# Ranks two steps behind the rows, logits' parts taken out of the bank by ScalarE, eight groups of row blocks, up to two row scatters a step, and the leading expert's weights asked for behind all of v

## The chip, the cores and the metric

The kernel runs on one core of a Trainium2 chip. The time is the device time of one execution in microseconds (us), the median of several runs. A profile is one further execution under the hardware profiler; its span, 430.7 us, goes from the first to the last instruction.

Names in the profile: PE is TensorE's matmuls, PEld its weight loads, DVE is VectorE, ACT is ScalarE, POOL is GpSimd, SP is SyncE, which here issues the loads. A "bank" is one of the eight banks of PSUM, the memory that TensorE writes.

## The reference

Gated linear attention first, one recurrence per batch and head, over 768 tokens with head dimension 48, for 4 batches and 8 heads:

```
state = alpha[t][:, None] * state + outer(k[t], v[t])
y[t]  = q[t] @ state
```

The results are laid out as 3072 rows of 384 numbers, `x`. Then comes a router with eight experts, of which each row takes one:

```
logits = normalised(x) @ normalised(expert_emb).T / tau
expert = argmax(logits);  gate = softmax(logits)[expert]
out[row] = gate * (relu(x[row] @ w1[expert]) @ w2[expert])
```

`w1` is 384 x 1024 and `w2` 1024 x 384 for each expert; everything is fp32.

## The kernel before

**Two stages.** The attention stage works in 24 chunks of 128 tokens (`NS` = 24, six to a batch). A pipelined loop of 27 steps `s` runs over them: step `s` starts chunk `s`, does the scores of chunk `s - 1`, and finishes chunk `s - 2`. The expert stage then goes through the experts in turn. The leading one is chosen at run time from those that have at least 256 rows after 16 chunks, so that its first 256 rows can be worked on early (`fetch_early`, `turn_early`, `first_layer_early`, in steps 24 to 26).

**A step.** `decays` transposes alpha, k and q on TensorE into banks (`pa`, `pk`, `pq`). VectorE scans alpha backwards (`r`, L480), multiplies k by it (`kr`, L487), and in `decay_queries` scans alpha forwards (`a`, L504). GpSimd multiplies q by that (`qs`, L508). `keys_back` turns `kr` of the chunk before back (`pkb`, then `kb` by ScalarE, L525). `scores` multiplies keys by queries and masks (VectorE one half; ScalarE copies the other, L573, and GpSimd masks it, L574). `decay_state` (`dec`, L533, GpSimd) and `update` (`pd`; `state`, L558, VectorE) carry the state on. The first chunk of each batch has no carried state, so two steps later TensorE has fewer products. `mix_states` and `mix_chunk` form the outputs by columns (`pyx`, then `ycols` by ScalarE, L613), and `rows` (L615) turns them into rows.

**Rows and logits.** In `rows` the matrix `sel` holds unit columns and the scaled expert embeddings, so the product `px` gives in one bank both the rows (2 x 48 columns in each of four parts) and the logits' parts (8 columns in each). VectorE adds the four parts up (L633), and ScalarE copies the rows (L637). Both write into `x`, a tile for a whole group of chunks; its columns from `LG` on are the logits, and column `TK` is the token's number.

**Banks.** `pa`, `pk`, `pq`, `pkb` and `px` share three banks (`ps_tr`). A product can start when a bank is free, which is when all who read the tile that was in it are done. `pd` and the ranks' product `rk` share one (`ps_mm`).

**Routing.** Chunks are gathered into groups (`GROUPS`). One step after the last rows of a group are due, so at the end of step `last + 2`, `choose` (L325) finds the expert of each row on VectorE: five operations over the group, then the running count `before`, one addition per chunk on GpSimd (L342), on VectorE for chunks 15 and 23. A step later, at `last + 3`, `place` (L344) gets the rank of each row among the rows of its expert: two products with a triangle and a matrix of ones into `rk`, a multiplication (L364), a sum (L366) and a conversion to whole numbers (L367), which gives `dest`. `to_rows` (L312) then scatters one chunk's rows to DRAM at `dest` by an indirect DMA that GpSimd issues (L313); `send` is the list of chunks that wait for it, and inside the loop one chunk a step is sent. After chunk 15, `place` also gives the counts to `first_expert` (L375), a chain of small VectorE operations that ends in `turn_i` and `row0`.

**Order.** TensorE's order is written out: `in_turn()` puts each product behind the last. `behind(s)` puts work behind the forward scan on VectorE and behind `qs` on GpSimd. The rest of each engine's order is fixed when the kernel is built, by a planner that goes by program order and its own estimates of when inputs are ready.

**Loads.** `load(s)` (L447) asks SyncE's queue for alpha, k and q of chunk `s` and v of chunk `s - 1`; it is called two steps ahead, and four buffers (five for v) limit how far transfers run ahead. `weights(i)` (L135) asks for the two matrices of the expert that is `i`-th in turn; it reads the number from `turn_i` first. `weights(0)` is asked for right after `fetch_early()`, behind the scatter of chunk 15, and `weights(1)` at step 23.

Of the kernel before, what the change touches and what calls it, by code (L numbers as in the profile page):

```python
# [9 lines left out]
FP32 = mybir.dt.float32  # L10
I32 = mybir.dt.int32
AF = mybir.ActivationFunctionType
ALU = mybir.AluOpType
AX = mybir.AxisListType
# [13 lines left out]
def kernel(  # L28
# [12 lines left out]
    nc = tc.nc  # L41
    B, H, S, D = q.shape
# [16 lines left out]
    LG, TK, ROW = DM, DM + E, DM + E + 1  # L59

    GROUPS = (
        (0, 3), (3, 6), (6, 9), (9, 12), (12, 14), (14, 16), (16, 19), (19, 21), (21, 23), (23, 24)
    )
    GMAX = max(b - a for a, b in GROUPS)

# [130 lines left out]
    def in_turn():  # L196
        return tc.issue_after(last["pe"].ins) if last else ExitStack()


    with ExitStack() as c1:  # L200
# [143 lines left out]
        def place(g, total=False):  # L344

            s0, s1 = GROUPS[g]
            n = s1 - s0
            ch = chosen[:, s0:s1]
            bank = ps_mm.tile([P, GMAX + 1, E], FP32, tag="mm", name="rk")
            rk = bank[:, 0:n]  # L350
            rkf = rk.rearrange("p s e -> p (s e)")
            mm(
                rkf, lhsT=ones, rhs=before[:, s0:s1].rearrange("p s e -> p (s e)"),
                start=True, stop=False,
            )
            mm(
                rkf, lhsT=earlier, rhs=ch.rearrange("p s e -> p (s e)"),
                start=False, stop=True,
            )
            if total:  # L360

                mm(bank[:, GMAX], lhsT=ones, rhs=before[:, s1], start=True, stop=True)
            at = work.tile([P, GMAX, E], FP32, name="at_row")[:, 0:n]
            nc.vector.tensor_tensor(at, rk, ch, ALU.mult)  # L364
            row = work.tile([P, GMAX], FP32, name="row")[:, 0:n]
            nc.vector.tensor_reduce(row.unsqueeze(2), at, axis=AX.X, op=ALU.add)  # L366
            nc.vector.tensor_copy(dest[:, s0:s1], row)  # L367
            send.extend(range(s0, s1))
            if not total:
                return None  # L370
            m = work.tile([P, E], FP32, name="n")
            nc.vector.tensor_tensor(m, bank[:, GMAX], ebase, ALU.subtract)
            return m
# [73 lines left out]
        def load(s):  # L447

            if s < NS:
                b, c = divmod(s, NCH)  # L450
                i = s % NBUF
                for p0, p1 in ((1, AROW), (AROW, P)):
                    nc.sync.dma_start(out=at_s[i][p0:p1, :, 0:D], in_=a_r[b, c, p0:p1])
                nc.sync.dma_start(out=kt_s[i][:, :, 0:D], in_=k_r[b, c])
                nc.sync.dma_start(out=qt_s[i][:, :, 0:D], in_=q_r[b, c])
            if s > 0:
                b, c = divmod(s - 1, NCH)
                nc.sync.dma_start(out=vt_s[(s - 1) % NBV][:, :, 0:D], in_=v_r[b, c])

        def behind(s):  # L460

            queue = ExitStack()
            for call in st[s]["last"]:
                queue.enter_context(tc.issue_after(call.ins))
            return queue
# [149 lines left out]
        def rows(s):  # L615

            yT = st[s]["yT"]
            px = ps_tr.tile([P, 2, NQ, 2 * D + E], FP32, tag="tr", name="px")
            for hh in range(2):
                for q in range(NQ):  # L620

                    for i in range(2):
                        sl = slice(i * HALF, (i + 1) * HALF)
                        mm(
                            px[sl, hh, q], lhsT=yT[hh][:, q, sl], rhs=sel[:, hh, q],
                            start=True, stop=True, skip_group_check=True,
                        )
            g = group_of[s]
            s0, s1 = GROUPS[g]
            if s == s0:  # L630
                x_g[g] = work.tile([P, GMAX, ROW], FP32, name="x", bufs=4)[:, 0 : s1 - s0]
            x = x_g[g][:, s - s0]
            nc.vector.tensor_reduce(  # L633
                x[:, LG : LG + E].unsqueeze(2), px[:, :, :, 2 * D :].rearrange("t a q e -> t e a q"),
                axis=AX.XY, op=ALU.add,
            )
            nc.scalar.copy(  # L637
                x[:, 0:DM].rearrange("t (q j a d) -> t a q j d", q=NQ, j=2, a=2),
                px[:, :, :, 0 : 2 * D].rearrange("t a q (j d) -> t a q j d", j=2),
            )  # L640


# [21 lines left out]
        def warm(n):  # L664

            pw = ps_mm.tile([P, P], FP32, tag="mm", name="pw")
            for _ in range(n):
                mm(pw, lhsT=ident, rhs=ident, start=True, stop=True)

        send = []  # L670
        warm(7)
        fixed_parts()
        load(0)
# [2 lines left out]
        load(1)  # L676
        for s in range(NS + 3):
            if s + 2 <= NS:
                load(s + 2)
            if 0 <= s - 1 < NS:  # L680
                with in_turn():
                    keys_back(s - 1)
            if s < NS:
                decays(s)
            if s == NS:
                with in_turn():
                    turn_early()
            if s < NS:
                decay_queries(s)
            if 0 <= s - 1 < NS:  # L690
                decay_state(s - 1)

                with in_turn(), tc.issue_after(st[s]["a_scan"].ins) if s < NS else ExitStack():
                    scores(s - 1)
            if s == 0:
                with behind(s), in_turn():
                    prepare_first(a0)
                with behind(s):
                    prepare_logits()
            if NS <= s < NS + 2:  # L700
                with in_turn():
                    first_layer_early(2 * (s - NS), 2 * (s - NS) + 1)
            if 0 <= s - 2 < NS:
                with in_turn():
                    mix_states(s - 2)
                with in_turn():
                    mix_chunk(s - 2)
            if 0 <= s - 1 < NS:

                with in_turn(), tc.issue_after(st[s]["a_scan"].ins) if s < NS else ExitStack():  # L710
                    update(s - 1)
            if 0 < s < NS and s % NCH == 0:

                with in_turn():
                    keys_back(s, ps_mm, "mm")
            if NS <= s < NS + 2:
                with in_turn():
                    first_layer_early(2 * (s - NS) + 1, 2 * (s - NS) + 2)
            if 0 <= s - 2 < NS:
                with in_turn():  # L720
                    rows(s - 2)
            if s == 1:
                with in_turn():
                    turn_logits()
            if s == 2:
                with behind(s):
                    routing_constants()
            if s == 3:
                with behind(s):
                    convert_constants()  # L730
            if 4 <= s < 4 + NXG * (NC + 1):
                i, t = divmod(s - 4, NC + 1)
                with behind(s):
                    nc.gpsimd.memset(xg_s[i][:, t], 0.0)
            if s == 3:
                with behind(s):
                    nc.gpsimd.memset(blank, 0.0)

            r = s - 3
            if r >= 0:  # L740
                g = group_of[r]
                if r == GROUPS[g][1] - 1:
                    with in_turn():
                        n = place(g, r in (S0 - 1, NS - 1))
                    if r == S0 - 1:
                        with behind(s):
                            first_expert(n)
            with behind(s) if s < NS else ExitStack():
                for c in send[:] if s >= NS else send[:1]:
                    to_rows(dest[:, c : c + 1], x_g[group_of[c]][:, c - GROUPS[group_of[c]][0]])  # L750
                    send.remove(c)
                    if c == S0 - 1:
                        fetch_early()
                        weights(0)
            if s == NS - 1:
                weights(1)
            r = s - 2
            if 0 <= r < NS:
                g = group_of[r]
                if r == GROUPS[g][1] - 1:  # L760
                    choose(g)
                    with behind(s) if s < NS else ExitStack():
                        nc.gpsimd.tensor_copy(x_g[g][:, :, TK], toks[:, slice(*GROUPS[g])])
            if s > NS:
                with in_turn():
                    first_layer_early(2 * (s - NS) + 2, 2 * (s - NS) + 4)
# [483 lines left out]
```

## Time and profile before

Three runs: 432.58, 432.67 and 433.79 us.

| what | value |
|---|---|
| median time | 432.67 us |
| span of the profile | 430.7 us |
| busy: PE, PEld | 412.2, 361.2 us |
| busy: DVE, ACT, POOL | 280.9, 174.6, 192.4 us |
| attention loop, first alpha transpose of chunks 0 to 23 | 4.7 to about 141.5 us |
| first early product of the leading expert | 149.25 us |
| TensorE's granted clock, mean | 0.996 |

Busy time is the sum of an engine's instructions, so TensorE's 412.2 of 430.7 us says that it has nearly always something in hand. Its matmuls are pipelined, and the ends shown are modelled; the weight loads, one before each product, are therefore the better clock of what it does. In the timeline, a line gives start and length in us, the engine, the line of the kernel, the operation, what it writes and reads, and how many instructions of the kind it merges; in brackets stands the idle time of the engine ahead of it, and what ended that. In the list of waits, a line gives the waiting engine with its operation, the one it waited for, the total in us, how often, and the longest.

### The profile page before, as it was taken

Reading aid. Unit: us, or ns where it says so; the run is one execution under the profiler, and the core shown is the slowest. Engines: PE = TensorE matmul, PEld = TensorE weight load, DVE = VectorE, ACT = ScalarE, POOL = GpSimd, SP = SyncE. Lnnn points to the kernel's source line nnn. Section 1 sums busy time; section 2 is a strip of 40 time slices with the busy share of each in tenths; the row PEclk is TensorE's granted clock in tenths of the full one; section 3 lists DMA queues with packets and bytes.
Section 4 is the critical chain, followed back from the end, with each engine's and each line's share of the span. In section 5 each row is a group of like instructions: output and inputs, shape, how many; then the busy total and the mean of one; then the engine's idle time right before and its main releaser. Section 6 shows DMA issues by size and latency. Waiting matters only on the chain. (4 is left out here: it accounts for less than half of the span.)

```text
span 430.7 us, 10669 instructions
## 1 busy us (share of the span) xinstructions
PE 412.2 (96%) x3970; PEld 361.2 (84%) x3970; DVE 280.9 (65%) x749; ACT 174.6 (41%) x406; POOL 192.4 (45%) x285
## 2 busy tenths in 40 slices
PE   7999999999989999999999999999999999999995
PEld 6888888888878877779899789798878979978984
DVE  7888778788788614854865856833781684693631
ACT  4444544444444434463532522522261352352410
POOL 7555777667655826911007118023601802702701
PEclk9999999999999999999999999999999999999998
DMA  9999899999957942868108209105602800001001
GB/s 139 158 167 161 179 183 190 192 187 198 185 111 216 389 148 94 260 224 317 66 16 299 101 21 350 38 37 186 200 19 70 320 2 36 21 0 49 4 17 38
DMA packets 119371, 60.15 MB, mean 140 GB/s; under 512 B 102287, under 2 KB 113816, under 8 KB 119312
## 3 DMA queue, kind: packets, MB, share of 16 engines
q1 hardware_dynamic: 115208, 49.14, 50.1%
q0 software_dynamic: 3728, 10.16, 6.7%
q8 instruction: 38, 0.62, 0.7%
q14 instruction: 21, 0.17, 0.1%
q10 hardware_dynamic: 376, 0.05, 0.1%
HBM read 49.69 MB, written 11.45 MB: 142 GB/s over the span
## 5 line engine op out<-in xcount | busy, mean ns | idle before, releaser
L805 POOL DMA_INDIRECT out_dram<-y,sx x25 | 24.3, 972 | 164.4 <-DVE xT_m L964 81.1
L987 PE MATMUL pq<-xT,w 128*128 128x192 f32 x280 | 64.4, 328 | 1.5 <-PEq L1148 0.7
L987 PEld LDWEIGHTS pq<-xT,w 128*128 128x128 f32 x280 | 47.3, 190 | 3.2 <-issue 2.5
L910 DVE TENSOR_TENSOR hT<-pq,v 128x192 f32<-128x192 f32 x84 | 29.9, 356 | 28.3 <-PE pq L987 25.9
L508 POOL TENSOR_TENSOR qs<-qc,a 128x512 f32<-128x512 f32 x24 | 30.7, 1279 | 33.6 <-DVE a L504 24.4
L894 PE MATMUL pyo<-w,hT 128*128 128x384 f32 x128 | 43.3, 492 | 0.0
L987 PE MATMUL pq<-xT_m,w_m 128*128 128x192 f32 x168 | 36.8, 328 | 1.5 <-ACTq L1148 1.2
L894 PEld LDWEIGHTS pyo<-w,hT 128*128 128x128 f32 x128 | 23.7, 190 | 15.3
L995 ACT ACTIVATE hT<-hT 128x384 f32<-128x384 f32 (+1 forms) x56 | 24.8, 443 | 24.9 <-DVE hT L910 20.2
L480 DVE TENSOR_TENSOR_SCAN r<-pa,inr 128x511 f32<-128x511 f32 x24 | 29.1, 1214 | 5.3 <-PE pa L194 5.1
L987 PEld LDWEIGHTS pq<-xT_m,w_m 128*128 128x128 f32 x168 | 28.7, 190 | 2.3 <-ACTq L1148 1.8
L313 POOL DMA_INDIRECT xs<-x,dest x24 | 24.8, 1032 | 11.3 <-DVE best L337 4.5
L504 DVE TENSOR_TENSOR_SCAN a<-pa,ini 128x512 f32<-128x512 f32 x24 | 29.3, 1222 | 0.7
L1035 PE MATMUL pq<-w_m,hT_m 128*128 128x192 f32 x168 | 29.6, 326 | 0.0
L934 POOL TENSOR_TENSOR w_m<-w 128x384 f32<-128x384 f32 x28 | 27.5, 1004 | 4.0 <-DMA out_dram<-y,sx 1.7
L910 DVE TENSOR_TENSOR v<-pq,v 128x192 f32<-128x192 f32 x56 | 20.0, 356 | 12.7 <-ACT v L998 5.6
L995 ACT ACTIVATE hT<-pq 128x192 f32<-128x192 f32 x28 | 9.3, 331 | 46.8 <-PE pq L987 46.8
L191 PE MATMUL sc<-qs,kr 64*128 64x128 f32 x384 | 27.9, 285 | 0.0
L1035 PEld LDWEIGHTS pq<-w_m,hT_m 128*128 128x128 f32 x168 | 27.7, 190 | 0.0
L934 POOL TENSOR_TENSOR w_m<-w,w_m 128x384 f32<-128x384 f32 x28 | 27.1, 996 | 0.0
L191 PEld LDWEIGHTS sc<-qs,kr 64*128 64x128 f32 x384 | 23.3, 187 | 4.0 <-issue 3.0
L191 PE MATMUL pyx<-sm,vt 128*64 128x128 f32 x384 | 26.3, 279 | 0.0
(199 smaller groups left out, 895.0 us busy)
## 6 DMA issues: line engine op xcount, KB each, us to landing
w<-in_moe_w_dram SPq DMA_DIRECT2D x16, 1536.0 KB
kt<-in_k_dram SPq DMA_DIRECT2D x24, 192.0 KB
qt<-in_q_dram SPq DMA_DIRECT2D x24, 192.0 KB
vt<-in_v_dram SPq DMA_DIRECT2D x24, 192.0 KB
xg<-xs SPq DMA_DIRECT2D x22, 196.5 KB
at<-in_alpha_dram SPq DMA_DIRECT2D x24, 168.0 KB
xg<-xs SPq DMA_DIRECT2D x8, 98.2 KB
at<-in_alpha_dram SPq DMA_DIRECT2D x24, 22.5 KB
```

The lines of the kernel that those rows point to most:

```text
L191: last["pe"] = nc.tensor.matmul(*args, **kwargs)
L313: ins = nc.gpsimd.indirect_dma_start(out=xs, out_offset=bass.IndirectOffsetOnAxis(ap=rows, axis=0), in_=x, in_offset=None, bounds_check=E ...
L480: nc.vector.tensor_tensor_scan(r[:, L - 2 :: -1], pa[:, L - 1 : 0 : -1], inr[:, L - 2 :: -1], 1.0, ALU.mult, ALU.add,)
L504: d["a_scan"] = by_dve = nc.vector.tensor_tensor_scan(a, pa, ini, 0.0, ALU.mult, ALU.add)
L508: by_pool = nc.gpsimd.tensor_tensor(qs.rearrange("p n t -> p (n t)"), d["qc"], a, ALU.mult)
L805: ins = nc.gpsimd.indirect_dma_start(out=out, out_offset=bass.IndirectOffsetOnAxis(ap=col, axis=0), in_=y, in_offset=None, bounds_check=N - 1,
L894: pe[:] = [nc.tensor.matmul(py, lhsT=hT[:, f], rhs=w2_t[:, f], start=(f == 0), stop=(f == FT - 1),)]
L910: dve[:] = [call(*args)]
L934: nc.gpsimd.tensor_tensor(to[:, f], x[:, f], y[:, f], ALU.subtract)
L987: pe[:] = [nc.tensor.matmul(to, lhsT=left, rhs=right, start=start, stop=stop, skip_group_check=True,)]
L995: return nc.scalar.activation(h, p, AF.Relu)
L1035: pe[:] = [nc.tensor.matmul(to, lhsT=left[:, f], rhs=right[:, f], start=start and f == 0, stop=stop and f == n - 1, skip_group_check=True,)]
```

## The change

Five edits.

1. The groups become longer and fewer: eight in place of ten. `place` writes `dest` as whole numbers out of the sum itself, so that the separate conversion goes.
2. `place` comes a step later for most groups, at `last + 4`, so that the counts of a group have a step to get ready before TensorE is to multiply them. Group (14, 16), which decides the leading expert, and the last two groups stay at `last + 3`. The dictionary `placed_at` says which groups are placed at the end of which step.
3. When more than two chunks wait in `send`, two are sent in a step in place of one.
4. ScalarE copies the logits' parts out of the bank into a small tile `lg`, and then the rows; VectorE adds the parts up from `lg`. So one engine alone reads the bank of `px`.
5. `weights(0)` moves to step 22, behind the load of the last v, in place of behind the scatter of chunk 15.

```diff
     GROUPS = (
-        (0, 3), (3, 6), (6, 9), (9, 12), (12, 14), (14, 16), (16, 19), (19, 21), (21, 23), (23, 24)
+        (0, 4), (4, 8), (8, 12), (12, 14), (14, 16), (16, 20), (20, 23), (23, 24)
     )
...
             nc.vector.tensor_tensor(at, rk, ch, ALU.mult)
-            row = work.tile([P, GMAX], FP32, name="row")[:, 0:n]
-            nc.vector.tensor_reduce(row.unsqueeze(2), at, axis=AX.X, op=ALU.add)
-            nc.vector.tensor_copy(dest[:, s0:s1], row)
+            with nc.allow_low_precision(reason="a whole number and zeros"):
+                nc.vector.tensor_reduce(dest[:, s0:s1].unsqueeze(2), at, axis=AX.X, op=ALU.add)
...
-                nc.sync.dma_start(out=vt_s[(s - 1) % NBV][:, :, 0:D], in_=v_r[b, c])
+                return nc.sync.dma_start(out=vt_s[(s - 1) % NBV][:, :, 0:D], in_=v_r[b, c])
...
-            nc.vector.tensor_reduce(
-                x[:, LG : LG + E].unsqueeze(2), px[:, :, :, 2 * D :].rearrange("t a q e -> t e a q"),
-                axis=AX.XY, op=ALU.add,
-            )
+
+            lg = work.tile([P, 2, NQ, E], FP32, name="lg", bufs=1)
+            nc.scalar.copy(lg, px[:, :, :, 2 * D :])
             nc.scalar.copy(
                 x[:, 0:DM].rearrange("t (q j a d) -> t a q j d", q=NQ, j=2, a=2),
                 px[:, :, :, 0 : 2 * D].rearrange("t a q (j d) -> t a q j d", j=2),
             )
+            nc.vector.tensor_reduce(
+                x[:, LG : LG + E].unsqueeze(2), lg.rearrange("t a q e -> t e a q"),
+                axis=AX.XY, op=ALU.add,
+            )
...
         send = []
+        placed_at = {}
+        for g, (_, s1) in enumerate(GROUPS):
+            soon = s1 == S0 or s1 > NS - 3
+            placed_at.setdefault(s1 + (2 if soon else 3), []).append(g)
...
             if s + 2 <= NS:
-                load(s + 2)
+                v_last = load(s + 2)
+            if s + 2 == NS:
+
+                with tc.issue_after(v_last.ins):
+                    weights(0)
...
-            r = s - 3
-            if r >= 0:
-                g = group_of[r]
-                if r == GROUPS[g][1] - 1:
-                    with in_turn():
-                        n = place(g, r in (S0 - 1, NS - 1))
-                    if r == S0 - 1:
-                        with behind(s):
-                            first_expert(n)
+            for g in placed_at.get(s, ()):
+                r = GROUPS[g][1] - 1
+                with in_turn():
+                    n = place(g, r in (S0 - 1, NS - 1))
+                if r == S0 - 1:
+                    with behind(s):
+                        first_expert(n)
             with behind(s) if s < NS else ExitStack():
-                for c in send[:] if s >= NS else send[:1]:
+                for c in send[:] if s >= NS else send[: 1 + (len(send) > 2)]:
                     to_rows(dest[:, c : c + 1], x_g[group_of[c]][:, c - GROUPS[group_of[c]][0]])
                     send.remove(c)
                     if c == S0 - 1:
                         fetch_early()
-                        weights(0)
```

## The prediction

> **What bounds the kernel now.** I read the page first, then the list of waits, then the timeline of TensorE's weight loads from 20 to 150 us, then all engines in one ordinary step, then GpSimd and VectorE alone. The page:
>
> ```profile
> PE 412.2 (96%) x3970; PEld 361.2 (84%) x3970; DVE 280.9 (65%) x749; ACT 174.6 (41%) x406; POOL 192.4 (45%) x285
> ```
>
> TensorE is the bound, in the attention stage (0 to about 147 us) as in the experts. The diff leaves the experts' code alone, so only time that TensorE loses before them can be won, and what is won there moves all that follows. An ordinary step takes 5.86 us (transposes of alpha start at 62.68 and 68.54). The list of waits shows who holds whom:
>
> ```profile
> ACT x L637 <- DVE x L633: 25.4, 24, 2.3
> ...
> DVE x L633 <- PE px L191: 13.5, 16, 4.8
> ...
> PEld pk L194 <- ACT x L637: 2.4, 2, 1.4
> ```
>
> Once in each of the 24 steps ScalarE's copy of the rows waits for VectorE's sum of the logits' parts out of the same bank, and twice TensorE waits for that copy. The weight loads of the long steps:
>
> ```profile
> 27.41 0.42 PEld L194 LDWEIGHTS pk<-ident,kt 128*128 128x128 f32 x4 [0.96 <-ACT x L637]
> ...
> 55.87 0.30 PEld L191 LDWEIGHTS rk<-before,ones 128*128 128x128 f32 x2 [1.07 <-issue]
> ...
> 91.65 0.30 PEld L191 LDWEIGHTS rk<-before,ones 128*128 128x128 f32 x2 [1.06 <-issue]
> ...
> 124.29 0.42 PEld L194 LDWEIGHTS pk<-ident,kt 128*128 128x128 f32 x4 [1.40 <-ACT x L637]
> ```
>
> At 27.41 and 124.29 the transposes of k want px's bank while VectorE is late (constants; the chain that finds the leading expert). At 55.87 and 91.65 it is the ranks' matmul: its bank is the one that the state was in, and VectorE, behind with `choose`, empties it only at 55.75 (state 55.34 + 0.41). Ordinary steps carry a small form of the first wait:
>
> ```profile
> 62.30 0.19 DVE L633 TENSOR_REDUCE x<-px 128x8 f32<-128x32 f32 x1 [0.22 <-PE px L191]
> 62.53 0.49 ACT L637 COPY x<-px 128x384 f32<-128x384 f32 x1 [0.98 <-DVE x L633]
> ...
> 62.93 0.59 ACT L525 COPY kb<-pkb 128x512 f32<-128x512 f32 x1
> 63.07 0.42 PEld L194 LDWEIGHTS pk<-ident,kt 128*128 128x128 f32 x4
> ...
> 63.57 0.42 PEld L194 LDWEIGHTS pq<-ident,qt 128*128 128x128 f32 x4
> ```
>
> pk starts 0.05 us after the row copy ends (63.02), pq 0.05 after the keys' copy ends (63.52); the same 0.05 stands at 68.92, 98.84 and 129.53. So ScalarE's chain, begun by VectorE, paces TensorE here a little.
>
> **What the Trainium skill says.** "Perfetto Trace Analysis", Identifying the Most-Contended Engine: judge TensorE by its weight loads rather than by matmul busy time; 84% here, and the gaps above show in them. "PSUM — Partial Sum Buffer", PSUM bank collisions: two engines must not touch one bank at once, reads included; the 24 waits agree. "ScalarE: Activation LUTs", What ACT_TABLE_LOAD costs: 186 ns plus 0.833 a column, neighbours overlapping by about 93. The trace: 586 ns at 512 columns, 484 at 384, so 0.80 a column, and the overlap is 0.09 (62.53 + 0.49 against 62.93). "SBUF — State Buffer", Who interferes with whom: a cast or an add of two SBUF inputs can be held by a GpSimd instruction, a reduce cannot. The trace: the cast at L367 takes 0.14 us at 40.53 and 0.48 at 104.99 beside a scatter.
>
> **Part by part.**
>
> Logits' parts by ScalarE. Added: 24 copies of 128x32. From the trace's fit, 484 - 352 x 0.80 = 0.20 us each, 4.9 us on an engine busy 4.8 of 10; the row copy can start 0.20 - 0.09 = 0.11 after it. Before, it started 0.27 after the last px product (62.26 to 62.53). ScalarE answers TensorE 0.04 to 0.12 later (phe, qc, sc), so the row copy starts 0.15 to 0.23 after it: 0.04 to 0.12 earlier; I take 0.08. About 13 steps are paced this way (those without ranks): 13 x 0.08 = 1.0 us, bounds 0.5 and 1.6. VectorE's reduce then waits for ScalarE, some 0.25 later, but 0.82 of idle follows it (r at 63.31 waits for pa); hidden.
>
> The bank is now freed by ScalarE alone, so both px waits go: 0.96 + 1.40 = 2.36. Does VectorE's lateness come back elsewhere? At 124 us it is 0.6 late on its next scan (123.65 against pa's end at about 123.05). What TensorE needs next from it: the alpha scan before the next pa, which ends at 66.67 for a pa at 68.44 in an ordinary step, 1.8 of slack; and kr before px, about 2 of slack. I take the whole 2.36.
>
> Fewer groups, ranks later. Inside the loop ranks fall behind steps 5, 8, 11, 14, 16, 18, 21, 23 before, and 7, 11, 15, 17, 18, 23 after. Two rank products fewer: a rank step adds 0.43 to 0.45 (133.65 to 137.13 is 3.48 against 2.84 at 61.31 to 64.15, less 0.19 of wait), so 0.88. The waits of 1.07 and 1.06 sat behind steps 8 and 14, short for TensorE (no carried state: 5.2 us) and just after `choose`. There are no ranks there now; beyond the usual 0.13 gap that is 1.87. Other rank gaps (0.23 to 0.32) save or cost 0.1.
>
> VectorE: 10 choose/place chains become 8, and 8 casts (0.14 to 0.48) go: some 3 us in all, off the path. A group of four adds one row's 8 columns to operations of about 0.18; hidden.
>
> Two scatters a step (7, 11, 15, 17, 18, 23). The second costs 1.02 plus 0.3 on GpSimd. Queued behind it:
>
> ```profile
> 62.75 1.02 POOL L313 DMA_INDIRECT xs<-x,dest  x1 [0.15 <-issue]
> 63.79 0.65 POOL L574 TENSOR_SCALAR_AFFINE_SELECT sm<-sm 128x512 f32<-128x512 f32 x1
> 64.39 0.62 POOL L533 TENSOR_TENSOR dec<-state,end 128x256 f32<-128x256 f32 x1
> ...
> 66.82 1.28 POOL L508 TENSOR_TENSOR qs<-qc,a 128x512 f32<-128x512 f32 x1 [1.65 <-DVE a L504]
> ```
>
> The masked scores (end 64.44) feed products at about 66.3: 1.8 of slack. The decayed state (65.01) is wanted by VectorE at 67.52: 2.5. qs has 1.65 idle ahead. So 1.3 fits; where the planner also makes GpSimd wait for the ranks first (0.8 to 1.0 at L313), it just about fits. Bounds for six steps: 0 to 6 x 1.3 = 7.8; I take 0.6.
>
> Leading weights earlier. Before they were asked for at 132.69, after the scatter of row block 15 (128.60); now right behind the last v (issued at about 127, later minus the gain). Their first product, at 149.25, waited for no transfer, so this hides nothing new: 0. The early rows (393 KB) may now queue behind 3 MB, about 9 us at the 389 GB/s of 140 to 150 us; they have 10 or more. Loads do not limit the loop: TensorE waited 0.3 us for q in all.
>
> The tail keeps its products. Three scatters instead of two after the last-but-one ranks (161.4 + 3 x 1.3 = 165.3) end before the last block's ranks let its scatter go (165.45). The two waits for the first expert's rows (0.47 and 1.06 at 172 to 174) move with all the rest: 0.
>
> Sum: 1.0 + 2.36 + 0.88 + 1.87 + 0.1 - 0.6 = 5.6; with 0.3 for rearrangements that I cannot see, 5.3. 432.67 - 5.3 = **427.4 us**.
>
> **Rivals.** (a) The waits move to the next need of VectorE: half of 2.36 + 1.87 comes back, and the pacing gives only its 0.5: 432.67 - 5.3 + 2.1 + 0.5 = 430.0. For: VectorE is 8 of 10 busy, and its order is the planner's. Against: the slacks of 1.8. (b) The second scatter stands ahead of masks and states in four of the six steps and costs 1.3 in each: 427.4 + 5.2 = 432.6, no change. For: in ordinary steps the scatter does stand ahead. Against: in rank steps (57.94, 136.58) masks and states went first. (c) It costs 1.3 in all six and the longer backlog delays the first expert's rows by two scatters (2.6), while TensorE has nothing else: 427.4 + 7.8 - 0.6 + 2.6 = 437.2, slower. Against: the slack of 1.8, and that 4 of the 6 are followed by steps with fewer scatters.
>
> **How the numbers follow.** Forecast 0.65, (a) 0.18, (b) 0.10, (c) 0.07. The low end is all bounds at their best, 5.6 + 0.6 + 0.6 = 6.8, so 425.8; the high end takes in (a) with some of the scatters' cost, 430.8. Faster 0.83, same 0.10, slower 0.07.
>
> **What would show it.** Right: no row copy waits for VectorE; no gap of about 1 us in the weight loads at steps 4, 8, 14, 20; pk less than 0.5 behind pa; six rank steps in the loop; the first-layer early products start some 5 us before 149.25, with the time from there to the end unchanged. Wrong: gaps of over 0.5 ahead of the products on masked scores or on qs in the six steps, or a longer wait for the first expert's rows.

## The result and the profile after

Beside the kernel before, the changed kernel was timed three times, on three occasions:

| occasion | changed, median (lowest to highest) | before | ratio, 95% interval |
|---|---|---|---|
| first, 4 runs | 429.0 (428.2 to 429.7) | 432.62 | 0.991, 0.9885 to 0.9934 |
| again, 4 runs | 426.0 (425.8 to 426.6) | 432.13 | 0.986, 0.9846 to 0.9875 |
| a third time, 5 runs | 426.28 (426.1 to 427.4) | 432.05 | 0.9863, 0.9846 to 0.988 |

It is faster in all three, by 3.6 and then by about 6 us; the forecast was 427.4, a gain of 5.3. (The third and the second occasion were on different chips; for the first the chip is not on record.) The first occasion stands apart, and part of the study below is about why.

The first profile after (span 427.9), busy times:

```profile
PE 412.1 (96%) x3962; PEld 363.6 (85%) x3962; DVE 276.6 (65%) x725; ACT 177.3 (41%) x430; POOL 191.7 (45%) x283
```

Eight matmuls fewer (two rank products of four instructions as counted here), 24 instructions fewer on VectorE, 24 more on ScalarE. The busy sums hardly move, so they can't show the gain. The list of waits does:

```profile
ACT lg L634 <- PE px L191: 17.0, 24, 0.8
...
DVE x L639 <- ACT lg L634: 11.7, 11, 5.7
```

The line in which ScalarE waited 24 times for VectorE is gone: ScalarE now waits for the product itself, and VectorE waits for ScalarE. An ordinary step, in the same profile:

```profile
61.84 0.19 ACT L634 COPY lg<-px 128x32 f32<-128x32 f32 x1 [0.81 <-PE px L191]
61.92 0.50 ACT L635 COPY x<-px 128x384 f32<-128x384 f32 x1
62.06 0.21 DVE L639 TENSOR_REDUCE x<-lg 128x8 f32<-128x32 f32 x1 [0.44 <-ACT lg L634]
62.11 0.47 PEld L194 LDWEIGHTS pa<-ident,at 128*128 128x128 f32 x4
62.42 0.59 ACT L524 COPY kb<-pkb 128x512 f32<-128x512 f32 x1
62.55 0.47 PEld L194 LDWEIGHTS pk<-ident,kt 128*128 128x128 f32 x4
...
63.06 0.42 PEld L194 LDWEIGHTS pq<-ident,qt 128*128 128x128 f32 x4
```

The row copy starts 0.08 after the small copy and ends 0.13 ahead of pk, so it no longer paces TensorE there. The keys' copy still does: it ends at 63.01, and pq starts at 63.06. The step is 5.81 us in place of 5.86.

The steps of the loop show the rest. Step `s` here lasts from the alpha transpose of chunk `s` to that of chunk `s + 1`. The first steps vary from execution to execution, so I count from chunk 4. "To early" runs from the alpha transpose of chunk 4 to the first early product of the leading expert (`phe`), which closes the part in which the time was won; the stretch from there to the leading expert's first second-layer product (`pyo`) has a row of its own.

| us, from the timelines | before | changed, first profile | again | third |
|---|---|---|---|---|
| alpha transpose of chunk 4 at | 26.09 | 27.20 | 26.09 | 27.25 |
| step 4 | 6.79 | 5.82 | 5.82 | 5.82 |
| step 8 | 6.63 | 6.15 | 5.21 | 5.22 |
| step 14 | 6.62 | 5.22 | 5.22 | 5.22 |
| step 16 | 6.41 | 6.18 | 5.81 | 5.81 |
| step 20 | 6.62 | 5.22 | 5.22 | 5.22 |
| chunk 4 to chunk 23 | 115.43 | 110.70 | 109.35 | 109.34 |
| to early | 123.16 | 118.36 | 117.01 | 117.00 |
| early product to first `pyo` | 17.34 | 18.04 | 17.34 | 17.34 |
| span | 430.7 | 427.9 | 424.5 | 425.3 |

Behind the first `pyo` come another 264.1, 264.3, 264.1 and 263.7 us. No edit below is to the experts' own code, yet in the other traces this stretch takes from 262.4 to 264.5 us (266.1 in one). So a difference of a us or two between two times can come from there, and I read what an edit is worth from the stretch "to early" first.

The long steps 4, 8, 14 and 20 are gone. Two executions of the changed kernel agree within 0.01 us from chunk 4 on: 6.15 us less than before. The first profile differs in three things. It starts 1.1 late, as the third also does: TensorE still runs at half speed there, as the transposes of k show in its timeline, which take 1.06 us and later 0.60 (the record of the clock shows it full from 14.4 us on, in the kernel before from 7.6):

```profile
10.97 1.06 PE L194 MATMUL pk<-ident,kt 128*128 128x128 f32 x4
...
16.55 0.60 PE L194 MATMUL pk<-ident,kt 128*128 128x128 f32 x4
```

It loses 1.35 in steps 8, 12 and 16 and 0.70 after the early product. Both of these come from waits for ScalarE, whose copies start late, here in step 8:

```profile
51.84 0.59 ACT L489 COPY qc<-pq 128x512 f32<-128x512 f32 x1 [0.80 <-PE pq L194]
54.13 0.59 ACT L572 COPY sm<-sc 128x512 f32<-128x512 f32 x1 [1.70 <-PE pyx L191]
```

The product that this copy waits for ended at about 52.84 by its record, but TensorE's completion signals, due from 52.84 on, are recorded at 53.31, 54.06, 54.15 and 54.24, in a burst. Such late signals stand at seven places of that trace before 171 us, each close behind row scatters that follow one another. The trace of the kernel before has one too, due at 152.00 and recorded at 152.51, behind the scatters at 149.74 and 151.07. That gave the first theory.

### The profile page after: what moved, and what is told of

Same layout as the page of the kernel before. It is cut to its first block, busy times and chain, and to the rows that moved or that the text cites. A ratio compares the mean times of both kernels' runs of the same rounds, so it can differ in the third digit from the quotient of the medians.

```text
span 427.9 us, 10636 instructions
## 1 busy us (share of the span) xinstructions
PE 412.1 (96%) x3962; PEld 363.6 (85%) x3962; DVE 276.6 (65%) x725; ACT 177.3 (41%) x430; POOL 191.7 (45%) x283
```

## Experiments

**First theory: the second scatter of a step holds TensorE's signals back.** One kernel takes three of the six pairs of scatters in the loop away, one adds six more.

```diff
-                for c in send[:] if s >= NS else send[: 1 + (len(send) > 2)]:
+                for c in send[:] if s >= NS else send[: 1 + (len(send) > 2 and s > 16)]:
```

> The changed kernel, with the second scatter of a step kept only from step 17 on (steps 7, 11 and 15 send one). Theory A (a row scatter issued directly behind another holds TensorE's completion signals back, so ScalarE starts its copies late and TensorE waits at the next products): the gaps of 0.82 us at 55.05, 0.17 and 0.23 at 78 and 0.23 at 101.63 go, 1.45 in all less about 0.2; 427.7 us beside 429.0. Theory B (those gaps come from the rank step with four chunks or from the order of the copies, not from the second scatter): they stay where they are, 428.7 to 429.3. In both the first expert's rows are asked for at the same step as before.

Measured: 426.27 us, 0.9849 (0.9828 to 0.987), below both theories' times.

```diff
+        def to_spare(j):
+            ins = nc.gpsimd.indirect_dma_start(
+                out=xd,
+                out_offset=bass.IndirectOffsetOnAxis(ap=spare[:, j : j + 1], axis=0),
+                in_=blank,
+                in_offset=None,
+                bounds_check=12 * P - 1,
+                oob_is_err=False,
+            )
...
+                if len(now) == 1 and s < NS:
+                    to_spare(len(spares))
+                    spares.append(s)
```

> The changed kernel, and in each of the six steps of the loop that send one chunk (8, 9, 12, 13, 16, 19) a second scatter directly behind it, of 128 blank rows into a DRAM tensor of its own that nobody reads. Theory A (TensorE's completion signals are held by the second of two scatters): late signals, in a burst, in most of these steps too, 0.2 to 0.8 us of TensorE's waiting each, 1.2 to 4.8 in all: 430.2 to 433.8 us. Theory B (only GpSimd's own queue counts, and it has over 1.3 us of slack in these steps): 428.8 to 429.4.

Measured: 427.01 us, 0.9867 (0.9845 to 0.9888). GpSimd's timeline in steps 8 and 9 of this kernel:

```profile
49.73 1.18 POOL L327 DMA_INDIRECT xs<-x,dest  x1 [0.17 <-issue]
51.21 0.98 POOL L327 DMA_INDIRECT xs<-x,dest  x1 [0.30 <-issue]
52.20 0.23 POOL L526 TENSOR_TENSOR end<-r,al 128x4 f32<-128x4 f32 x1
...
54.78 1.03 POOL L327 DMA_INDIRECT xs<-x,dest  x1 [0.16 <-issue]
55.82 0.65 POOL L587 TENSOR_SCALAR_AFFINE_SELECT sm<-sm 128x512 f32<-128x512 f32 x1
56.65 0.98 POOL L315 DMA_INDIRECT xd<-blank,spare  x1 [0.17 <-issue]
```

The pair at 49.73 and 51.21 is the same as in the first profile, and the new one at 56.65 comes on top. It does not stand directly behind the other, as the expectation has it: in all six places the mask of the scores went between. The test of the theory is therefore the pairs that stand as they stood in the first profile (49.73, and those at 72.73 and 95.30). No signal of TensorE is late, here or with fewer pairs; from chunk 4 to chunk 23 the two kernels take 109.32 and 109.34 us. The theory falls: such a pair alone does not delay the signals. A second scatter costs nothing that shows in the loop; the 0.7 by which the times of this kernel lie above the other's arise elsewhere, and I did not find out where.

**The changed kernel itself, twice more.**

> The changed kernel itself once more, for a second trace and beside the others on one chip. Theory A (what the first profile of it showed in the loop, TensorE waiting 0.82, 0.23 and 0.23 us for ScalarE at 55.05, 78.61 and 101.63 with TensorE's signals late, belongs to that one execution): no late signals, no such gaps, the loop from step 4 to step 23 at 109.3 us as in the kernels with fewer and with more scatter pairs, and 426.5 to 427.5 in the times. Theory B (it belongs to this order of the work): the gaps are there again, 110.7 from step 4 to step 23, 428.7 to 429.3.

Measured: 426.0 us; no late signals, 109.35 us. Theory A holds in the loop; the time is half a us below what it gave.

> The changed kernel a third time, since its first four times (428.2 to 429.7) and the four beside the second batch (425.8 to 426.6) lie 3 us apart. Theory A (the first four are the ones that stand apart: half the TensorE clock at the start and late signals): 425.8 to 426.8 us. Theory B (the kernel has two levels that depend on the chip or the loading of the program): near 429 on this chip or mixed.

Measured: 426.28 us, again Theory A, though this execution too started 1.1 late. So the late signals do not belong to the kernel: up to 172 us, only two of the fourteen traces have a signal that is more than 0.25 us late, the first of the changed kernel and that of the kernel before. What made them late, and why the other three times of the first occasion, of which there is no trace, were above 428 as well, stays open; the chip of that occasion is not ruled out.

**ScalarE's copy of the logits' parts, taken away and alone.**

```diff
-            lg = work.tile([P, 2, NQ, E], FP32, name="lg", bufs=1)
-            nc.scalar.copy(lg, px[:, :, :, 2 * D :])
+            nc.vector.tensor_reduce(
+                x[:, LG : LG + E].unsqueeze(2), px[:, :, :, 2 * D :].rearrange("t a q e -> t e a q"),
+                axis=AX.XY, op=ALU.add,
+            )
             nc.scalar.copy(
...
-            nc.vector.tensor_reduce(
-                x[:, LG : LG + E].unsqueeze(2), lg.rearrange("t a q e -> t e a q"),
-                axis=AX.XY, op=ALU.add,
-            )
```

> The changed kernel with the logits' sum read from the PSUM bank by VectorE again and no copy of the parts by ScalarE; groups, placing, scatters and weights stay changed. The prediction's terms: 0.08 us in each of 13 steps and the two waits of 0.96 and 1.40 for VectorE come back, 3.4 in all: 432.4 us. Rival: the eight groups and their later placing had already taken VectorE off the row copy's way, and only the pacing comes back, 1.0: 430.0. Second rival: ScalarE's extra copy costs as much as it saves, 429.0.

Measured: 429.33 us, 0.9925 (0.9905 to 0.9944): 3.2 above the 426.1 that the changed kernel takes on the later occasions, and 4.16 more to the early product. (The expected times stand on the 429.0 of the first occasion; the differences are what counts. Behind the first `pyo` this traced execution was 1.7 shorter than the changed kernel's second.) The prediction's 3.4 is the nearest of the three expectations. The waits of the row copy are back, in the weight loads of this kernel:

```profile
27.71 0.42 PEld L194 LDWEIGHTS pk<-ident,kt 128*128 128x128 f32 x4 [1.22 <-ACT x L637]
91.00 0.42 PEld L194 LDWEIGHTS pk<-ident,kt 128*128 128x128 f32 x4 [0.63 <-ACT x L637]
...
122.98 0.42 PEld L194 LDWEIGHTS pk<-ident,kt 128*128 128x128 f32 x4 [1.40 <-ACT x L637]
```

The reverse, the same edit put into the kernel before:

> The kernel before with the parts of the logits copied out of the bank by ScalarE alone of all edits; ten groups, one scatter a step and the weights' place as before. The prediction's terms: 1.0 for the pacing and 2.36 for the two waits of the row copy: 432.6 - 3.4 = 429.2 us, and the gaps of about 1.06 us at the rank products of steps 8 and 14 stay. Rival: these too end once the row copy no longer waits, 427.2. Second rival: the pacing alone, 431.6.

Measured: 433.18 us, 1.0019 (1.0005 to 1.0034): no gain at all, which none of the three expectations had. The times spread from 431.4 to 435.1 and the traced execution is the fastest; what the slower ones lose on top is not shown. Steps 4 and 20 are 0.98 and 1.40 shorter, as expected. But the weight loads show what was won being lost again:

```profile
55.21 0.30 PEld L191 LDWEIGHTS rk<-before,ones 128*128 128x128 f32 x2 [1.11 <-issue]
74.04 0.30 PEld L191 LDWEIGHTS rk<-before,ones 128*128 128x128 f32 x2 [1.07 <-issue]
91.64 0.30 PEld L191 LDWEIGHTS rk<-before,ones 128*128 128x128 f32 x2 [1.09 <-issue]
104.63 0.30 PEld L191 LDWEIGHTS rk<-before,ones 128*128 128x128 f32 x2 [1.05 <-issue]
...
147.11 0.30 PEld L191 LDWEIGHTS rk<-before,ones 128*128 128x128 f32 x2 [1.25 <-issue]
```

Where the kernel before had two such waits (55.87 and 91.65), this one has five. The matmul view names whom the one at 74.07 waits for:

```profile
74.07 0.37 PE L191 MATMUL rk<-before,ones 128*128 128x24 f32 x2 [0.89 <-DVE state L558]
```

In steps 8 and 14, at 55.21 and 91.64, this is the wait that was there before: VectorE is as late as it was. In steps 11 and 16, at 74.04 and 104.63, it is new, and VectorE itself is later. VectorE's timeline in step 11, first of the kernel before, where the step starts at 68.54:

```profile
69.12 0.52 DVE L334 TENSOR_TENSOR win<-x,top 128x24 f32<-128x24 f32 x1
69.56 1.21 DVE L480 TENSOR_TENSOR_SCAN r<-pa,inr 128x511 f32<-128x511 f32 x1
```

Then with the copy alone, where it starts at 67.78:

```profile
68.22 0.71 DVE L334 TENSOR_TENSOR win<-x,top 128x24 f32<-128x24 f32 x1
68.96 0.68 DVE L335 TENSOR_TENSOR win<-win,first 128x24 f32<-128x24 f32 x1
69.57 1.21 DVE L480 TENSOR_TENSOR_SCAN r<-pa,inr 128x511 f32<-128x511 f32 x1
```

The order that is fixed at build now puts two of the long operations of `choose` ahead of the backward scan in place of one. So the scan starts 1.79 us into the step and not 1.02, the state follows at 5.73 and not 4.96, and steps 11 and 16 are each some 0.77 longer. The changed kernel has this order in step 10 (scan at 1.80), but no rank product there waits for the state, and the step takes 5.82 us. The wait at 147.11 stands behind the loop, where the stretch from chunk 23 to the early product takes 1.05 more than before. The copy alone thus loses what it wins: two waits for VectorE stay, and new ones come, at least two of them from VectorE's order.

**The later placing, alone and taken away.** Alone, with the two scatters a step that go with it:

```diff
+        placed_at = {}
+        for g, (_, s1) in enumerate(GROUPS):
+            soon = s1 == S0 or s1 > NS - 3
+            placed_at.setdefault(s1 + (2 if soon else 3), []).append(g)
...
+            for g in placed_at.get(s, ()):
...
-                for c in send[:] if s >= NS else send[:1]:
+                for c in send[:] if s >= NS else send[: 1 + (len(send) > 2)]:
```

> The kernel before with the later placing (three steps behind instead of two) and up to two scatters a step, and nothing else of the change: ten groups, the logits summed from the bank by VectorE, weights as before. The prediction's terms: the two waits of 1.07 and 1.06 at rank products go, the row copy's waits of 0.96 and 1.40 stay: 2.0 faster than the kernel before, 430.2. Rival (each edit alone only moves the wait to VectorE's next need): 0 to 0.5 faster, and the row copy's waits grow.

Measured: 432.49 us, 1.0002 (0.999 to 1.0015). The rival has the number: the two waits at the rank products do go, and others come, in the weight loads:

```profile
56.70 0.42 PEld L194 LDWEIGHTS pk<-ident,kt 128*128 128x128 f32 x4 [0.66 <-ACT x L637]
91.81 0.42 PEld L194 LDWEIGHTS pk<-ident,kt 128*128 128x128 f32 x4 [0.44 <-ACT x L637]
116.45 0.30 PEld L191 LDWEIGHTS rk<-before,ones 128*128 128x128 f32 x2 [1.54 <-POOL before L342]
124.55 0.42 PEld L194 LDWEIGHTS pk<-ident,kt 128*128 128x128 f32 x4 [1.05 <-ACT x L637]
```

The first two lie one step behind the places where the rank products had waited, and the last is the row copy's old wait: these are VectorE's next need, as the rival has it. The third, the largest, is not. It is the rank product of group (14, 16), which does not move, and it waits for GpSimd's running count, here in the kernel before:

```profile
115.76 0.21 POOL L342 TENSOR_TENSOR before<-before,chosen 128x8 f32<-128x8 f32 x1
116.11 1.02 POOL L313 DMA_INDIRECT xs<-x,dest  x1
```

and with the later placing:

```profile
115.15 1.01 POOL L313 DMA_INDIRECT xs<-x,dest  x1 [0.16 <-issue]
116.19 0.21 POOL L342 TENSOR_TENSOR before<-before,chosen 128x8 f32<-128x8 f32 x1
```

A row scatter now stands ahead of the count (and on VectorE the masks ahead of `chosen`, which is counted), and step 18 is 1.40 us longer. That is the order fixed at build once more; without it the placing alone would be worth some 1.8 us to the early product (an estimate, 0.37 + 1.40), near the prediction's 2.0. No run shows that kernel.

Taken away from the changed kernel:

```diff
-            placed_at.setdefault(s1 + (2 if soon else 3), []).append(g)
+            placed_at.setdefault(s1 + 2, []).append(g)
```

The expectations here and above count steps from the group's last chunk; counted from the step in which its rows are due it is one step in place of two.

> The changed kernel with each group's rank product two steps behind its last rows' step, as in the kernel before, in place of three; eight groups and ScalarE's copy stay. Theory A (the rank product in the step in which VectorE also chooses waits for VectorE's state, as at 74.07 and 104.66 in the kernel with ScalarE's copy alone): waits of about 0.9 us in the five groups that move, 3 to 4.5 slower than the changed kernel. Theory B (the prediction's: only the two waits of 1.07 and 1.06 come back): 1.9 slower. Theory C (with fewer groups no rank product waits): 0.

Measured: 431.79 us, 0.9999 (0.9985 to 1.0012), 5.8 above the changed kernel on that occasion: the whole gain is gone. To the early product it takes 4.97 more, in the slowest of its fourteen executions, the one that is traced. From the weight loads:

```profile
44.81 0.40 PEld L191 LDWEIGHTS rk<-before,ones 128*128 128x128 f32 x2 [1.83 <-POOL before L342]
...
69.33 0.30 PEld L191 LDWEIGHTS rk<-before,ones 128*128 128x128 f32 x2 [0.41 <-issue]
92.83 0.30 PEld L191 LDWEIGHTS rk<-before,ones 128*128 128x128 f32 x2 [1.17 <-issue]
```

Theory A comes nearest, but the cost is above its 3 to 4.5, and the places are not all as it said: of the five groups that move three have a wait, and the largest, at 44.81, is for GpSimd's running counts. Behind that one TensorE ran at half clock for 3.4 us (the last section), which is up to 1.7 of the 4.97, an estimate: half of 3.4. It is the chain of `choose` and counts that is too short of time by a step, on whichever engine its end lies.

The lengths of the steps put these four kernels between the one before and the changed one; a cell that is long for its row is a wait or a rank product, which adds about 0.44:

| step | before | placing alone | copy alone | all but copy | all but placing | changed |
|---|---|---|---|---|---|---|
| 4 | 6.79 | 6.99 | 5.81 | 7.03 | 5.82 | 5.82 |
| 6 | 5.60 | 6.10 | 5.60 | 5.64 | 8.10 | 5.62 |
| 8 | 6.63 | 5.33 | 6.64 | 5.22 | 5.22 | 5.21 |
| 9 | 5.87 | 6.93 | 5.82 | 5.89 | 5.82 | 5.82 |
| 11 | 5.95 | 5.38 | 6.72 | 5.85 | 5.33 | 5.79 |
| 14 | 6.62 | 5.24 | 6.63 | 5.25 | 6.70 | 5.22 |
| 15 | 5.87 | 6.71 | 5.82 | 7.23 | 5.81 | 6.26 |
| 16 | 6.41 | 5.87 | 7.17 | 5.87 | 6.28 | 5.81 |
| 18 | 6.47 | 7.87 | 6.47 | 6.45 | 6.68 | 6.45 |
| 20 | 6.62 | 6.27 | 5.22 | 6.62 | 5.22 | 5.22 |
| to early | 123.16 | 122.79 | 123.28 | 121.17 | 121.98 | 117.01 |

(Steps 7, 10 and 22, not in this table, are 0.83, 0.72 and 0.57 longer without the placing than in the changed kernel, step 7 through the half clock.) To the early product, the copy alone wins nothing (-0.12), the placing alone 0.37; in the presence of the other edits the copy wins 4.16 and the placing 4.97. The parts that the order and the half clock have in these numbers are named above.

**The size of the groups.**

```diff
-        (0, 4), (4, 8), (8, 12), (12, 14), (14, 16), (16, 20), (20, 23), (23, 24)
+        (0, 3), (3, 6), (6, 9), (9, 12), (12, 14), (14, 16), (16, 19), (19, 21), (21, 23), (23, 24)
```

> The changed kernel with the ten groups of the kernel before; the later placing, ScalarE's copy and the rest stay. The prediction's term: two rank products more at 0.44 us, 0.9 slower than the changed kernel, all of it in the loop. Rival: the later placing depends on the larger groups (VectorE's chain of choosing comes more often and meets the rank products again), so waits of about 0.9 us for the state come back at several rank products: 3 to 4 slower.

Measured: 426.04 us (425.9 to 429.4), 0.9883 (0.9859 to 0.9908). From chunk 4 to chunk 23 it takes 110.24 us, 0.89 more than the changed kernel, just the term of the prediction; to the early product 0.44 more, and from there to the first `pyo` 0.45 (17.79 against 17.34). No waits come back, so the rival falls. The times do not show it: behind the first `pyo` the traced execution is 1.5 shorter than the changed kernel's, and the spread of 3.5 us is too wide to say more.

**One scatter a step.**

```diff
-                for c in send[:] if s >= NS else send[: 1 + (len(send) > 2)]:
+                for c in send[:] if s >= NS else send[:1]:
```

> The changed kernel with one scatter a step again; chunk 15 then leaves in step 22 and not in step 19, and more chunks wait for the end of the loop. The prediction's reading (two a step make up for the later placing, or the first expert's rows come late): the early transposes of the first expert's rows wait for their load, 1 to 4 us slower than the changed kernel. Rival (the rows' load has more than three steps of slack): 0, within 0.5.

Measured: 430.07 us, 0.9935 (0.9909 to 0.9962), 3.8 above the changed kernel on that occasion; its eleven times go from 427.4 to 431.4. The prediction's reading holds. The loop is the same (109.33); behind it TensorE waits for the first expert's rows:

```profile
143.70 0.87 PE L194 MATMUL pxe<-ident,xg 128*128 128x128 f32 x6 [2.37 <-DMA xg<-xs]
144.50 2.00 PE L191 MATMUL sc<-qs,kr 64*128 64x128 f32 x16
146.44 2.33 PE L191 MATMUL phe<-exT,w 128*128 128x256 f32 x6
```

To the first `pyo` this execution takes 4.15 us more. The wait is 2.37 of that; the scores' 2.00 us (1.16 at full clock) belong to another 3.4 us at half clock, 1.7 by the same estimate.

**The weights' place, taken away and alone.**

```diff
-            if s + 2 == NS:
-
-                with tc.issue_after(v_last.ins):
-                    weights(0)
...
                         fetch_early()
+                        weights(0)
```

> The changed kernel with the first two experts' leading weights asked for behind the scatter of chunk 15 again, ahead of the last loads of q and v. The prediction: 0, within 0.5 us. Rival: the last step's loads wait behind 1.5 MB of weights and TensorE waits at the last transposes, 1 to 2 us slower.

(The expectation speaks of two experts and 1.5 MB; the edit moves the two matrices of the leading one, 1536 KB each.) Measured: 427.62 us, 0.9903 (0.9889 to 0.9917), 1.6 above the changed kernel on that occasion, and 1.71 more to the early product: the rival. In step 23 TensorE waits for the last k and q:

```profile
136.88 0.63 PE L194 MATMUL pk<-ident,kt 128*128 128x128 f32 x4 [0.82 <-DMA kt<-in_k_dram]
...
138.05 0.63 PE L194 MATMUL pq<-ident,qt 128*128 128x128 f32 x4 [0.54 <-DMA qt<-in_q_dram]
```

The reason is in SyncE's timeline of this kernel; `w` are the weights:

```profile
122.05 0.41 SPq L181 DMA_DIRECT2D xg<-xs  x1
123.33 0.39 SPq L141 DMA_DIRECT2D w<-in_moe_w_dram  x1
123.95 0.38 SPq L144 DMA_DIRECT2D w<-in_moe_w_dram  x1
124.44 1.64 SPq L453 DMA_DIRECT2D kt<-in_k_dram  x1
126.17 4.97 SPq L454 DMA_DIRECT2D qt<-in_q_dram  x1
```

In the kernel before, the rows were fetched at 131.78 and the weights asked for from 132.69 on, when the last loads had long been issued (v at 120.97). With chunk 15 scattered earlier in the loop's work, the same line of code puts the weights ahead of them.

> The kernel before with the leading weights asked for behind the last load of v, and nothing else of the change. Theory A (the last loads of k and q stood just behind the weights and were hidden only because the loop was slow): no change, within 0.4 of 432.2, while the same edit is worth 1.4 to 1.6 in the changed kernel. Rival (it is worth as much here): 430.6.

Measured: 432.16 us, 1.0005 (0.9994 to 1.0015): nothing, Theory A.

## Why the prediction was right

The forecast held, and so did its mechanism: the time was won in the loop, by TensorE's waits, and all that follows moved with it. By its own steps:

- *Pacing by the row copy, 1.0:* mis-sized. Of the steps without ranks in either kernel, 9, 10 and 22 are 0.05 to 0.06 shorter, and 6, 12, 13 and 19 by 0.01 at most; with the steps that changed ranks it is some 0.3 in all. The row copy did start 0.08 after the small copy (0.11 was worked out), but the keys' copy behind it still ends 0.05 ahead of pq.
- *Other rank gaps, 0.1:* mis-sized the other way. Beyond the 0.44 for a rank product that moved, steps 5, 11, 16 and 21 are 0.08, 0.17, 0.16 and 0.24 shorter, 0.65 in all: the small gaps ahead of their rank products (0.24 at 74.03, 0.23 at 103.92, 0.32 at 134.71) were waits as well, and went. That this makes up for the pacing is luck.
- *The two px waits, 2.36:* steps 4 and 20 are 0.97 and 1.40 shorter, 2.37.
- *Two rank products fewer, 0.88:* 0.89 between chunks 4 and 23 by the kernel with ten groups.
- *The waits of 1.07 and 1.06, counted as 1.87:* steps 8 and 14 are 1.42 and 1.40 shorter; less 0.44 for the product that left them, 1.94.
- *Second scatters, -0.6:* mis-sized; six more of them left the loop at 109.32 us. The reading of GpSimd's queue, that the slack of 1.8 and 2.5 us behind the scatter takes it in, held.
- *Weights earlier, 0:* the step that failed. It asked whether the weights' own first product had waited, not what would stand behind the weights in the queue once chunk 15 left earlier. The edit is worth 1.6 here, as a guard. As the sum counted no wait for loads either, the total was not touched.
- *The tail, 0:* 17.34 us from the early product to the first `pyo`, before and after.

The terms came to 6.2 before the two deductions (0.6 for scatters, 0.3 unseen); 6.15 was measured to the early product. The first occasion's smaller gain is no term of the sum: its trace has 1.1 at the start, 1.35 and 0.70 for late signals, 3.2 of the 3.4 by which its span exceeds the 424.5 of the next.

Rivals (b) and (c), the scatters, fell. Rival (a), that waits move to VectorE's next need, fell for the whole change, yet it is part of what happens to either of its two main edits alone; the other part is the order of VectorE and GpSimd, which came out differently in those kernels (steps 11 and 16 with the copy, step 18 with the placing). The prediction rejected (a) on the slack of ordinary steps. What the runs show is that the change moves both of VectorE's deadlines at once, the bank of `px` and the rank products in the steps in which it also chooses, and this the prediction did not say; nor did it see that the copy makes VectorE later in such steps. Adding the terms as if each edit earned its own was right in the sum and wrong in the parts: the copy was priced at 3.36 and won nothing on its own, and removing the placing, whose waits were priced at 1.97, cost 5.8.

## What to carry to other kernels

When one engine is late in certain steps, list everything that the busiest engine needs from it in those steps and in the next; an edit that takes one need away hands the wait to the next, and the gain shows only when the last is gone. So an edit that measures as nothing by itself is not yet shown to be worth nothing. Where the order of the engines is fixed anew at each build, compare it too: an edit can lose its gain to an instruction that changed places far away. When an edit brings a transfer's trigger forward, read the queue it enters for what then stands behind it.

## What the runs showed of the hardware

In three places a long wait of TensorE was followed by one stretch of 3.4 us at half clock. In the kernel with the placing taken away it waited 1.63 us (to 44.81), and four transposes then took 1.06 us and not 0.60:

```profile
44.81 0.54 PE L191 MATMUL rk<-before,ones 128*128 128x32 f32 x2 [1.63 <-POOL before L342]
...
46.47 1.06 PE L194 MATMUL pk<-ident,kt 128*128 128x128 f32 x4
```

The granted clock was 0.51 from 44.9 to 48.3. The same followed a wait of 2.29 in the experts of that execution (from 396.5 on) and the wait of 2.37 us in the kernel with one scatter (half clock from 144.6 on). From chunk 4 on, waits of up to 1.40 us were not followed by it. The Trainium skill, "TensorE: Matmul & The Clock Gate", HAM oscillation — how this bites in real kernels, sets the limit at idle gaps of over some 3.4 us; here 1.63, with smaller gaps near it, was enough, and the measurement decides. A long wait thus costs more than its length.

The length of one wait is not all that counts. Three executions had such a stretch near their start, from 8.9 to 9.4 us on, with no single wait of over 0.8 us ahead of it from 4 us on: the changed kernel's second, the one with ten groups, and the kernel before with the weights moved. And in each trace the changes of the clock lie whole multiples of 3.41 us apart: in the kernel with the placing taken away at 7.40, 44.94, 48.36, 396.52 and 399.93, which is 11, 1, 102 and 1 of them. So where a wait falls between these points may matter as well; no run here tests that.
